# Gated attention and a bilinear feed-forward on one core: the gate applied per token at the end instead of being folded into the feed-forward and the attention sums

## The chip, the core and the metric

One Trainium2 chip, one of its cores. The time is the device time of one execution in microseconds (us), the median of several runs; lower is better. The core has five engines that run their own instruction streams and meet by semaphores: TensorE (PE, matrix products into PSUM), VectorE (DVE), ScalarE (ACT), GpSimd (POOL) and SyncE (SP, which here only issues DMAs).

## The reference

For 2048 tokens of width 512 the output mixes two branches by a sigmoid gate of the token:

```python
x = A_x
g = _sigmoid((x * gate_w).sum(-1, keepdims=True))
a = _A_ref(x, A_wqkv, A_wo)                      # attention, 32 heads of 16
b = _B_ref(x, B_w_gate, B_w_up, B_w_down)        # ((x @ w_gate) * (x @ w_up)) @ w_down
return g * a + (1 - g) * b
```

The feed-forward's inner width F is 1376, eleven column blocks of 128 (the last of 96).

## The kernel before, in words

**Attention.** The queries are cut into four chunks c of 512, the heads into eight groups of four heads per chunk, so there are NG = 32 groups m = (c, b, p), and each has 16 key tiles kt of 128: 512 *entries* (m, kt) of four *heads* each. For a head PE makes 128 keys x 512 queries of scores in one PSUM bank (L950), some engine exponentiates them to bf16, and PE multiplies the four heads of an entry with the values into psO (L1189, "PV"); a column of ones beside the values gives the softmax's denominators. PSUM has eight banks: psS is six of them, used as two slots of three, psO one, psX one; the sixth bank of psS also serves as a second general bank.

**Two engines exponentiate.** ACT takes spans of two or three banks with one Exp (L1551) and writes to a ring PT. DVE takes whole entries whose kt is in DK (five key tiles of a group at most): for each head a clamp to int16 out of PSUM (L1082, four per entry, into a *buffer* of four heads), then four "cheap" passes over the whole buffer (L1111), each giving an approximate exponential at another offset; PE multiplies each of the four with values that POOL has scaled by another weight (VD, and wv once it has been used; L569), so such an entry costs four PVs. Pass k = 3 is written in place, and the buffer is free again when its PV is done. There are two buffers in I2 (part of tile SC) and a third: bsb at first, and wk once the last key projection has read wk (lines with `third`, `bsb_i`, `wk_i`; `nb = (dst["buf"] + 1) % 3` in `d_claim`). No entry goes to DVE before the model time D_START = 38.

**The rest of PE's work is units** (class `Unit`): a chain of matmuls into one general bank and a drain of that bank, mostly by DVE. Units wait in `fills`, sorted by a due time counted in entries begun. There are projections of keys (`mk_k`), queries (`mk_q`), values (`mk_v`), one unit for the gate's 64 tiny products (`mk_gate`, due 16), the feed-forward's `mk_ug` (per chunk c and column block f one unit "u" and one "g", multiplied into hT), and `mk_dw`: for a tile of 128 tokens t of the first three chunks, eleven matmuls of hT with w_down and four of the attention's output OT with wo in one accumulation, drained by one copy to ost (L782) and stored. The last chunk uses `mk_d` (L728, a copy to bsb) and four tail units with `combine` (L747). FFN gives the due times chunk by chunk.

**How the gate gets there.** ACT and DVE make gval = g and omg = 1 - g, [128 x 16], token t*128 + p in partition p and column t. For folding them into operands they must lie along the free dimension, so POOL stores both to DRAM, gsc, one element of 4 bytes at a time (L626, two DMAs of 8 KB), reads g back as gC (L638, eight DMAs) and 1 - g as omgB, broadcast to all partitions, 512 tokens at a time (L587; later chunks from SP). The drain of a "u" unit multiplies by omgB (L674). The softmax's reciprocal denominators are multiplied by gC (L1284, in `finish`), which therefore waits until gC is there.

**The ends of a pair of groups.** `norm` copies psO to oraw (L1244) and issues on SP four DMAs to onum (L1251) and one of the denominators to den (L1261). `finish` lets DVE make reciprocals (L1280), SP write and broadcast them through DRAM into rb (L1294, L1307) and POOL multiply (L1310) into OT; `o_mult` is that product. `mk_q` after its drain (L504) issues eight DMAs on SP (L513), Qst to QX, 16 KB each, which lay the heads' queries apart; the scores of the next head block b wait for them.

**What sets the order.** Nothing reorders at run time: each engine follows its program, and a wait holds all that stands behind it. The program is made ahead by a greedy simulation in the kernel's text (`_Plan`, `step_pe`, `step_act`, `step_dve`) with assumed durations (`dur`, `lat`): at each step PE takes scores, PVs or a unit, DVE takes from `dve_q` by priority what the simulation holds ready, and `d_claim` gives DVE an entry when the simulation finds DVE not too far behind. So how many entries DVE takes follows from how busy the simulation thinks it is.

Of the kernel before, what the change touches and what calls it, by code (L numbers as in the profile page):

```python
# [151 lines left out]
def _build(nc, A_x, A_wqkv, A_wo, W_gate, W_up, W_down, gate_w, out):  # L152
# [10 lines left out]
    NB = 4  # L163
# [5 lines left out]
    D_START = 38.0  # L169
    X_FILL = 45.0  # L170
# [11 lines left out]
    FFN = [(64, 160, 164, 5), (184, 270, 275, 5), (295, 385, 395, 4), (412, 478, 480, 5)]  # L182
# [7 lines left out]
    gsc = nc.dram_tensor("gscr", [2, S], F32, kind="Internal").ap()  # L190

    with ExitStack() as stack:
# [28 lines left out]
        bsb = sb("bsb", [128, 4, D], BF16)  # L221
        omgB = sb("omgB", [128, 512], F32)
        gC = sb("gC", [128, NCH, 32], F32)
# [310 lines left out]
        def mk_v(t, due):  # L534
# [3 lines left out]
            def drain(un, last):  # L538
# [24 lines left out]
                def make():  # L563
                    un.free = P.op("dve", lambda v: v.tensor_copy(vf[:], un.bank), deps, **EV)
                    for k in range(4):
                        dst_ = hc((VV[:, t, :] if k == 0 else vdk(t)[:, k - 1, :])[:, 0 : 17 * H])
                        o = P.op(
                            "pool",
                            lambda g, k=k, dst_=dst_: g.tensor_scalar(dst_, hd(vf[:]), _WT[k], None, ALU.mult),  # L569
                            [un.free, o_vd, o_one],  # L570
                            dur=1.3,
                        )
                        if k == 0:
                            ev_v[t] = o
                    ev_vd[t] = o
# [5 lines left out]
        ogate, o_omg, gate_wait = {}, {}, []  # L581

        def ld_omg(c, deps, eng="sp"):

            o_omg[c] = P.dma(
                eng,
                lambda e: e.dma_start(omgB[:], bass.AP(gsc.tensor, gsc.offset + S + 512 * c, [[0, 128], [1, 512]])),  # L587
                deps,
                f"domg{c > 0}",
            )  # L590


        def mk_gate(due):
# [13 lines left out]
            def drain(un, last):  # L607
                def amake():
                    e1 = un.free = P.op(
                        "act",  # L610
                        lambda a: a.activation(gex[:], un.bank[:, 0:T], ACT.Exp, scale=-1.0),
                        [last],
                        dur=0.1,
                        lat=0.15,
                    )

                    def make():
                        e2 = P.op("dve", lambda v: v.tensor_single_scalar(gden[:], gex[:], 1.0, ALU.add), [e1])
                        e3 = P.op("dve", lambda v: v.reciprocal(gval[:], gden[:]), [e2], dur=0.2)
                        ogate["g"] = P.op(  # L620
                            "dve", lambda v: v.tensor_scalar(omg[:], gval[:], -1.0, 1.0, ALU.mult, ALU.add), [e3]
                        )
                        for i, src_ in enumerate([gval, omg]):
                            o = P.dma(
                                "pool",
                                lambda e, i=i, src_=src_: e.dma_start(  # L626
                                    gsc[i].rearrange("(t p) -> p t", p=128), src_[:], allow_slow_non_contiguous=True
                                ),
                                [ogate["g"]],
                                "dgs",  # L630
                                dur=1.0,
                                lat=20.0,
                            )
                        for i in range(8):
                            p, j = i % 2, i // 2
                            o1 = P.dma(
                                "pool",
                                lambda e, p=p, j=j: e.dma_start(  # L638
                                    gC[32 * j : 32 * j + 32, :, 16 * p : 16 * p + 16],
                                    bass.AP(gsc.tensor, gsc.offset, [[16, 32], [512, NCH], [1, 16]]),  # L640
                                ),
                                [o],
                                "dgc",
                                dur=1.0,
                            )
                        ogate["c"] = o1
                        for dl in gate_wait:
                            dl[-1] = o1
                        ld_omg(0, [o], "pool")

                    dve_push(3, [e1], make)

                act_q.append(([last], amake))
# [3 lines left out]
        def mk_ug(c, f, which, due):  # L657
# [9 lines left out]
            def drain(un, last):  # L667
                if which == "u":
                    deps = [last, u_free.get(n - 2), o_omg[c]]

                    def make():
                        ev_u[n] = un.free = P.op(
                            "dve",
                            lambda v: v.tensor_tensor(usb[0:w, n % 2, :], un.bank[0:w, :], omgB[0:w, :], ALU.mult),  # L674
                            deps,
                            **EV,
                        )
                        if f == FT - 1 and c < NCH - 1:
                            ld_omg(c + 1, [un.free])
# [18 lines left out]
            def deps():  # L698
                r = [d_wu if which == "u" else d_wg] + xdep(c)
                if which == "u":  # L700
                    r.append(o_omg[c])
# [12 lines left out]
        def mk_d(c, tt, due):  # L714
# [6 lines left out]
            def drain(un, last):  # L721
# [3 lines left out]
                deps = [last, last_v.get("b")]  # L725

                def make():
                    ev_b[t] = un.free = P.op("dve", lambda v: v.tensor_copy(bsb[:, tt, :], un.bank), deps, **EV)  # L728
# [3 lines left out]
            def deps():  # L732
                r = [d_wd] + [ev_h[c, f] for f in range(FT)]
                return r
# [5 lines left out]
        def combine(t, bank, last, un=None, dst=None):  # L740
# [3 lines left out]
            def make():  # L744
# [3 lines left out]
                        dst, bank, gval[:, t : t + 1], bsb[:, t % 4, :], ALU.mult, ALU.add  # L748
# [16 lines left out]
        def mk_dw(c, tt, due):  # L765

            t = 4 * c + tt

            def mm(pe, bk, i, s0, s1):
                if i < FT:  # L770
                    w = FW[i]
                    return cmm(pe, bk, hT[0:w, i, tt * 128 : (tt + 1) * 128], wd[0:w, i, :], s0, s1)
                b = i - FT
                return cmm(pe, bk, OT[:, c % 2, b, tt * 128 : (tt + 1) * 128], wo[:, b, :], s0, s1)

            def drain(un, last):
                if tt == 3:
                    ot_use[c] = h_use[c] = last
                deps = [last, o_out.get(t - 2)]

                def make():
                    o_comb[t] = un.free = P.op("dve", lambda v: v.tensor_copy(ost[:, t % 2, :], un.bank), deps, **EV)  # L782
                    o_out[t] = P.dma(
                        "sp",
                        lambda e: e.dma_start(out2[t * 128 : (t + 1) * 128, :], ost[:, t % 2, :]),
                        [o_comb[t]],
                        f"dout{t % 2}",
                    )

                dve_push(2, deps, make)  # L790

            def deps():
                r = [d_wd, d_wo] + [ev_h[c, f] for f in range(FT)] + [o_mult[c, b] for b in range(NB)]
# [4 lines left out]
            return Unit(due, chain(FT + NB, mm), deps, drain)  # L798
# [87 lines left out]
        def cap(sl, now):  # L886


            if sl and not xs[1]["res"] and now > X_FILL:
# [102 lines left out]
        bsb_i = bsb[:, :, :].bitcast(I16)  # L992
        third = {}

        def i2b(e):


            return I2[:, on_d[e], :, :] if on_d[e] < 2 else third[e]
# [10 lines left out]
        def d_claim(now):  # L1009
            if now < D_START or not last_x or tails or l_state["n"] > D_CHEAP:  # L1010
                return False
            nb = (dst["buf"] + 1) % 3
# [21 lines left out]
            if nb == 2:  # L1034
                third[g, kt] = wk_i if "k" in last_v else bsb_i
# [33 lines left out]
        def d_unit(j, bank, o, h):  # L1069
# [5 lines left out]
            d4 = [o, d_free[nb] or (last_x[0] if nb < 2 else None)]  # L1075
            if nb == 2 and third[e] is wk_i:
                d4.append(last_v["k"])

            def make():
                x = P.op(  # L1080
                    "dve",
                    lambda v: v.tensor_scalar(i2b(e)[:, j, :], bank, _LO, _HI, ALU.max, ALU.min),  # L1082
# [14 lines left out]
        def cheap(e, nb):  # L1097
# [5 lines left out]
            def mk(k):  # L1103
                lf = l_free[k] if k < 3 else None

                def make():
                    src = i2b(e)[:, :, :].rearrange("p a b -> p (a b)")
# [44 lines left out]
        def lview(e, k, j):  # L1152
            nb = on_d[e]
            return (LL[:, k, j, :] if k < 3 else i2b(e)[:, j, :]).bitcast(BF16)
# [11 lines left out]
        def do_pv(it):  # L1166
# [45 lines left out]
            if isd:  # L1212
                if k == 3:
                    nb = on_d[e]
                    d_free[nb] = o
                    if nb == 2 and third[e] is bsb_i:
                        last_v["b"] = o
# [57 lines left out]
        def finish(blk, c, b, dd, nd, half):  # L1275
# [3 lines left out]
            def make():  # L1279
                r = P.op("dve", lambda v: v.reciprocal(rec[:, s, 0:w_], den[:, s, 0:w_]), dd + [norm_ops.get(("scr", blk - 2))], dur=0.25)  # L1280
                if c < NCH - 1:
                    r = P.op(
                        "dve",
                        lambda v: v.tensor_tensor(rec[:, s, 0:w_], rec[:, s, 0:w_], gC[:, c, 0:w_], ALU.mult),  # L1284
                        [r, ogate["c"]],
                    )
# [30 lines left out]
            dl = dd + [ogate.get("c", "pending")]  # L1317
            if "c" not in ogate:
                gate_wait.append(dl)
            dve_push(1, dl, make)  # L1320


# [5 lines left out]
        fl.append((16, mk_gate(16)))  # L1328
# [8 lines left out]
        for c, (a0, a1, ad, dd) in enumerate(FFN):  # L1337
            for f in range(FT):
                for i, w in enumerate("ug"):
                    du = a0 + (a1 - a0) * (2 * f + i) / (2 * FT)  # L1340
                    fl.append((du, mk_ug(c, f, w, du)))
            for tt in range(4):
                du = ad + dd * tt
                fl.append((du, (mk_dw if c < NCH - 1 else mk_d)(c, tt, du)))
# [74 lines left out]
        def step_pe():  # L1419
# [41 lines left out]
            if xi is not None:  # L1461
                f = pick_fill(t + 0.3)
                if t > X_FILL and any(isinstance(x["u"], Unit) for x in xs):
# [215 lines left out]
```

## Time and profile before

| | |
|---|---|
| median of 3 runs | 779.12 us (777.76 to 781.05) |
| the profiled execution's own time | 779.12 us |
| its span, first to last instruction | 777.4 us (1.7 us lie around it) |
| mean granted TensorE clock | 0.968 of full |
| busy: PE, DVE, ACT, POOL | 715.6, 697.9, 729.7, 75.1 us |
| ACT's Exp, 128x1024 and 128x1536 | 434 and 235 times, mean 1074 and 1500 ns |
| DVE's clamps (L1082) and cheap passes (L1111) | 464 and 464 times, mean about 690 and 710 ns |
| DMA moved | 23.95 MB in 33745 packets, 20756 of them under 512 B |

The heads divide into 464 on DVE (116 entries) and 1584 on ACT. The mean of an instruction is longer than its share of time when the next one begins before it ends: in a row of DVE's 128x512 drains starts lie 0.60 us apart, at a mean duration of about 0.69 us. In a timeline row the two numbers are the start and the duration in us; the bracket at the end is the engine's idle time before it and what released it. SPq is the SP engine's issuing of DMAs.

### The profile page before, as it was taken

The numbers are of one execution on the slowest core, as the hardware profiler recorded it, in microseconds if no ns is written. First come the engines' busy times: TensorE is split into PE (matmuls) and PEld (weight loads), VectorE is DVE, ScalarE is ACT, GpSimd is POOL, SyncE is SP. The second block draws the span as 40 slices with busy tenths as digits, with TensorE's granted clock in tenths as the row PEclk, the third lists the DMA queues.
The fourth block names the chain that finished last, engine by engine and source line by source line (L and its number), as shares of the span: only waits on it lengthen the run. The fifth ranks groups of instructions, "written<-read, shape, count | busy, mean of one in ns | idle before, by whom it ended". The sixth has DMA issues, their size and how long they took to land.

```text
span 777.4 us, 21121 instructions
## 1 busy us (share of the span) xinstructions
PE 715.6 (92%) x8982; PEld 212.3 (27%) x8982; DVE 697.9 (90%) x1164; ACT 729.7 (94%) x680; POOL 75.1 (10%) x84
## 2 busy tenths in 40 slices
PE   9993898999899899999999999999887999999997
PEld 3330222222222222222222222222221322222234
DVE  3382999999999899999998999999998999999865
ACT  6982999999999989999998999999997999999995
POOL 8862000000001000000000000000000000000000
PEclk9986999999999999999997999999998999999999
DMA  8863010001010010101001010000101001000001
GB/s 175 272 11 23 8 30 13 17 11 30 9 29 22 16 30 22 30 8 24 16 11 35 14 40 19 23 17 9 27 18 29 16 23 32 14 19 14 24 11 42
DMA packets 33745, 23.95 MB, mean 31 GB/s; under 512 B 20756, under 2 KB 27988, under 8 KB 33652
## 3 DMA queue, kind: packets, MB, share of 16 engines
q1 hardware_dynamic: 31908, 21.21, 11.9%
q0 software_dynamic: 688, 1.13, 1.0%
q8 instruction: 72, 1.18, 0.7%
q10 hardware_dynamic: 1056, 0.26, 0.2%
q14 instruction: 21, 0.17, 0.1%
HBM read 12.35 MB, written 2.37 MB: 19 GB/s over the span
## 4 chain that ended last, share of the span: by engine, by line
DVE 41%; PE 34%; ACT 12%; DMA 4%; SPq 3%; issue 3%; POOL 1%; DVEq 0%; ACTq 0%
DVE SC L1111 15%; ACT PT L1551 12%; PE psS L950 11%; DVE SC L1082 11%; PE psX L374 10%; PE psO L1189 10%; DVE wk L1082 5%; SPq L1251 3%; DVE usb L674 2%; DMA den<-oraw 2%; DMA QX<-Qst 2%; DVE hT L691 2%; DVE oraw L1244 1%; DVE bsb L1082 1%; PE psS L374 1%
## 5 line engine op out<-in xcount | busy, mean ns | idle before, releaser
L1551 ACT ACTIVATE PT<-psS 128x1024 bf16<-128x1024 f32 (+1 forms) x670 | 721.9, 1222 | 32.3 <-PE psS L950 26.5
L950 PE MATMUL psS<-QX,KT 32*128 32x512 bf16 x1991 | 274.0, 391 | 39.1 <-ACT PT L1551 15.2
L1111 DVE TENSOR_SCALAR SC<-SC 128x2048 int16<-128x2048 int16 x308 | 206.3, 709 | 4.4 <-remote 2.4
L1082 DVE TENSOR_SCALAR SC<-psS 128x512 int16<-128x512 f32 x273 | 183.0, 687 | 17.4 <-PE psS L950 16.7
L950 PEld LDWEIGHTS psS<-QX,KT 32*128 32x128 bf16 x1991 | 69.5, 91 | 303.7 <-ACT PT L1551 86.2
L1189 PE MATMUL psO<-PT,VV 128*32 128x512 bf16 x1518 | 147.9, 393 | 1.1 <-DVE oraw L1244 0.6
L1189 PE MATMUL psO<-SC,VD 128*32 128x512 bf16 x1208 | 115.0, 395 | 6.2 <-DVE SC L1111 5.3
L1310 POOL TENSOR_TENSOR OT<-onum,rb 128x512 bf16<-128x512 f32 x16 | 23.4, 1464 | 664.0 <-DMA rb<-rscr 664.0
L1082 DVE TENSOR_SCALAR wk<-psS 128x512 int16<-128x512 f32 x113 | 75.8, 687 | 6.0 <-PE psS L950 5.5
L1111 DVE TENSOR_SCALAR SC<-wk 128x2048 int16<-128x2048 int16 x96 | 64.4, 689 | 2.9 <-PE psS L1199 1.6
L374 PE MATMUL psX<-wd,hT 128*32 128x512 bf16 (+1 forms) x704 | 57.8, 392 | 2.4 <-DVE ost L782 1.9
L374 PE MATMUL psX<-xT,wu 128*32 128x512 bf16 x688 | 53.1, 388 | 1.1 <-DVE wk L1082 0.5
L374 PE MATMUL psX<-xT,wg 128*32 128x512 bf16 x688 | 52.8, 388 | 0.7 <-DVE SC L1082 0.2
L1189 PEld LDWEIGHTS psO<-PT,VV 128*32 128x32 bf16 x1518 | 38.2, 96 | 53.6 <-issue 39.8
L1189 PE MATMUL psO<-SC,VV 128*32 128x512 bf16 x456 | 45.6, 390 | 1.2 <-DVE SC L1111 0.9
L1189 PEld LDWEIGHTS psO<-SC,VD 128*32 128x32 bf16 x1208 | 29.9, 95 | 58.7 <-DVE SC L1111 32.9
L691 DVE TENSOR_TENSOR hT<-psX,usb 128x512 bf16<-128x512 f32 (+1 forms) x44 | 30.2, 686 | 0.7 <-PE psX L374 0.7
L674 DVE TENSOR_TENSOR usb<-psX,omgB 128x512 bf16<-128x512 f32 (+1 forms) x44 | 30.2, 687 | 0.2 <-PE psX L374 0.2
L1082 DVE TENSOR_SCALAR SC<-psX 128x512 int16<-128x512 f32 x35 | 24.0, 687 | 0.8 <-PE psX L1052 0.6
L1111 DVE TENSOR_SCALAR wk<-wk 128x2048 int16<-128x2048 int16 x32 | 23.9, 747 | 0.0
L1244 DVE COPY oraw<-psO 128x512 f32<-128x512 f32 x31 | 21.3, 688 | 0.7 <-PE psO L1189 0.7
L1052 PE MATMUL psX<-QX,KT 32*128 32x512 bf16 x55 | 21.6, 393 | 0.1
(131 smaller groups left out, 399.7 us busy)
## 6 DMA issues: line engine op xcount, KB each, us to landing
rb<-rscr SPq DMA_DIRECT2D x16, 256.0 KB
onum<-oraw SPq DMA_DIRECT2D x124, 32.0 KB, 2.0
QX<-Qst SPq DMA_DIRECT2D x120, 16.0 KB, 1.8
out_dram<-ost SPq DMA_DIRECT2D x12, 128.0 KB, 1.7
wu<-in_B_w_up_dram SPq DMA_DIRECT2D x1, 1376.0 KB, 7.0
wg<-in_B_w_gate_dram SPq DMA_DIRECT2D x1, 1376.0 KB, 9.9
wd<-in_B_w_down_dram SPq DMA_DIRECT2D x1, 1280.0 KB, 12.5
omgB<-gscr SPq DMA_DIRECT2D x3, 256.0 KB, 3.4
```

Of the source, the lines that this page charges most:

```text
L374: r = pe.matmul(dst_[j : j + 32, :], lhs[:, j : j + 32], rhs, start=s0, stop=s1, tile_position=(0, j), skip_group_check=True,)
L674: lambda v: v.tensor_tensor(usb[0:w, n % 2, :], un.bank[0:w, :], omgB[0:w, :], ALU.mult),
L691: lambda v: v.tensor_tensor(hT[0:w, f, :], un.bank[0:w, :], usb[0:w, n % 2, :], ALU.mult),
L950: q = pe.matmul(bank_ap(sl, k_), KT[32 * j : 32 * j + 32, b, kt * 128 : (kt + 1) * 128], QX[32 * j : 32 * j + 32, p, b, :], start=True, st ...
L1052: lambda pe: pe.matmul(bank, KT[32 * j : 32 * j + 32, b, kt * 128 : (kt + 1) * 128], QX[32 * j : 32 * j + 32, p, b, :], start=True, stop=True,
L1082: lambda v: v.tensor_scalar(i2b(e)[:, j, :], bank, _LO, _HI, ALU.max, ALU.min),
L1111: lambda v: v.tensor_scalar(dstt, src, 0.5, _BASE + _OFF[k], ALU.mult, ALU.add),
L1189: r = pe.matmul(psO[r_, :], vcol(m, kt, k_, j), pj, start=first, stop=last, tile_position=(0, 32 * j), skip_group_check=True)
L1244: o_ev[m] = P.op("dve", lambda v: v.tensor_copy(oraw[:, s, :], psO[:]), deps, **EV)
L1251: lambda e, r0=r0: e.dma_start(onum[r0 : r0 + 16, :], oraw[r0 : r0 + 16, s, :]),
L1310: lambda g: g.tensor_tensor(OT[:, c % 2, b, :], onum[:], rb[:], ALU.mult),
L1551: lambda a: a.activation(cell_ap(cells[0], n).rearrange("p a b -> p (a b)"), bank_ap(sl, 0, n), ACT.Exp, scale=_LN2 / _OCT,),
```

## The change

The gate is no longer folded into operands. gsc, gC, omgB, their DMAs, the multiplication by gC and the wait for it are gone. The drain of "u" is a plain copy. Every chunk uses `mk_d`, whose drain multiplies by 1 - g, taken per token from omg, into bsb, now a ring of five tiles; for the first three chunks a new unit `mk_wo` multiplies OT with wo (four matmuls), and `combine` drains it as gval * bank + bsb into ost. With it go: bsb is no third buffer for DVE's entries, so there are two until wk is free; D_START is 45 in place of 38 (X_FILL, from which the second general bank is given up, stays at 45 under that name); the gate unit is due at 20 in place of 16; the feed-forward's due times are spread evenly from 60 to 490; the simulation's assumed duration of POOL's value scaling (L569) is 0.75 in place of 1.3.

```diff
-    D_START = 38.0
-    X_FILL = 45.0
+    D_START = 45.0
...
-    FFN = [(64, 160, 164, 5), (184, 270, 275, 5), (295, 385, 395, 4), (412, 478, 480, 5)]
+    FFN_FROM, FFN_TO = 60.0, 490.0
...
-    gsc = nc.dram_tensor("gscr", [2, S], F32, kind="Internal").ap()
...
-        bsb = sb("bsb", [128, 4, D], BF16)
-        omgB = sb("omgB", [128, 512], F32)
-        gC = sb("gC", [128, NCH, 32], F32)
+        bsb = sb("bsb", [128, 5, D], BF16)
...
-                            dur=1.3,
+                            dur=0.75,
...
-                        for i, src_ in enumerate([gval, omg]):
-                            o = P.dma(
-                                "pool",
-                                lambda e, i=i, src_=src_: e.dma_start(
-                                    gsc[i].rearrange("(t p) -> p t", p=128), src_[:], allow_slow_non_contiguous=True
-                                ),
-                                [ogate["g"]],
...
-                        for i in range(8):
-                            p, j = i % 2, i // 2
-                            o1 = P.dma(
-                                "pool",
-                                lambda e, p=p, j=j: e.dma_start(
-                                    gC[32 * j : 32 * j + 32, :, 16 * p : 16 * p + 16],
...
-                        ld_omg(0, [o], "pool")
...
-                    deps = [last, u_free.get(n - 2), o_omg[c]]
+                    deps = [last, u_free.get(n - 2)]
...
-                            lambda v: v.tensor_tensor(usb[0:w, n % 2, :], un.bank[0:w, :], omgB[0:w, :], ALU.mult),
...
+                            "dve", lambda v: v.tensor_copy(usb[0:w, n % 2, :], un.bank[0:w, :]), deps, **EV
...
-                deps = [last, last_v.get("b")]
+                deps = [last, ogate["g"], b_use.get(t - 5)]
                 def make():
-                    ev_b[t] = un.free = P.op("dve", lambda v: v.tensor_copy(bsb[:, tt, :], un.bank), deps, **EV)
+                    ev_b[t] = un.free = P.op(
+                        "dve",
+                        lambda v: v.tensor_scalar(bsb[:, t % 5, :], un.bank, omg[:, t : t + 1], None, ALU.mult),
+                        deps,
+                        dur=0.65,
+                        lat=0.1,
+                    )
...
-        def mk_dw(c, tt, due):
+        def mk_wo(c, tt, due):
             t = 4 * c + tt
-            def mm(pe, bk, i, s0, s1):
-                if i < FT:
-                    w = FW[i]
-                    return cmm(pe, bk, hT[0:w, i, tt * 128 : (tt + 1) * 128], wd[0:w, i, :], s0, s1)
-                b = i - FT
+            def mm(pe, bk, b, s0, s1):
                 return cmm(pe, bk, OT[:, c % 2, b, tt * 128 : (tt + 1) * 128], wo[:, b, :], s0, s1)
             def drain(un, last):
                 if tt == 3:
-                    ot_use[c] = h_use[c] = last
-                deps = [last, o_out.get(t - 2)]
...
+                    ot_use[c] = last
+                combine(t, un.bank, last, un)
             def deps():
-                r = [d_wd, d_wo] + [ev_h[c, f] for f in range(FT)] + [o_mult[c, b] for b in range(NB)]
+                r = [d_wo, ev_b[t]] + [o_mult[c, b] for b in range(NB)]
...
-            return Unit(due, chain(FT + NB, mm), deps, drain)
+            return Unit(due, chain(NB, mm), deps, drain)
...
-            nb = (dst["buf"] + 1) % 3
+            nb = (dst["buf"] + 1) % (3 if "k" in last_v else 2)
...
-                if c < NCH - 1:
-                    r = P.op(
-                        "dve",
-                        lambda v: v.tensor_tensor(rec[:, s, 0:w_], rec[:, s, 0:w_], gC[:, c, 0:w_], ALU.mult),
-                        [r, ogate["c"]],
-                    )
...
-        fl.append((16, mk_gate(16)))
+        fl.append((20, mk_gate(20)))
...
-        for c, (a0, a1, ad, dd) in enumerate(FFN):
+        n_ffn = NCH * (2 * FT + 4)
+        a0, a1 = FFN_FROM, FFN_TO
+        q = 0
+        for c in range(NCH):
             for f in range(FT):
-                for i, w in enumerate("ug"):
-                    du = a0 + (a1 - a0) * (2 * f + i) / (2 * FT)
+                for w in "ug":
+                    du = a0 + (a1 - a0) * q / n_ffn
                     fl.append((du, mk_ug(c, f, w, du)))
+                    q += 1
             for tt in range(4):
-                du = ad + dd * tt
-                fl.append((du, (mk_dw if c < NCH - 1 else mk_d)(c, tt, du)))
+                du = a0 + (a1 - a0) * q / n_ffn
+                fl.append((du, mk_d(c, tt, du)))
+                q += 1
+        for c in range(NCH - 1):
+            fl += [(128 * (c + 1) + 8 + 3 * tt, mk_wo(c, tt, 128 * (c + 1) + 8 + 3 * tt)) for tt in range(4)]
```

## The prediction, on record before the changed kernel ran

> **What bounds the kernel now.** I began with the page: busy times, then the 40 slices.
>
> ```profile
> span 777.4 us, 21121 instructions
> PE 715.6 (92%) x8982; PEld 212.3 (27%) x8982; DVE 697.9 (90%) x1164; ACT 729.7 (94%) x680; POOL 75.1 (10%) x84
> ...
> DVE  3382999999999899999998999999998999999865
> ACT  6982999999999989999998999999997999999995
> PEclk9986999999999999999997999999998999999999
> ```
>
> Three engines are near full. The digits say where they are not: the filling, the tail, and one hole in slice 4 (58 to 78 us), where both DVE and ACT stand at 2 and the clock at 6. Outside, DVE and ACT share the exponentials and are full together, so work added to DVE is paid by giving ACT heads. So two questions: what makes the hole, and what does the change do to the balance?
>
> For the hole I took the timelines by engine, then the waits from 58 to 80 us.
>
> ```profile
> 51.37 1.16 POOL L626 DMA_DIRECT2D gscr<-omg  x1
> ...
> 53.81 5.01 SPq L513 DMA_DIRECT2D QX<-Qst  x8
> ...
> 70.25 0.57 POOL L638 DMA_DIRECT2D gC<-gscr  x1 [17.73 <-DMA gscr<-omg]
> ...
> 71.64 0.61 PE L950 MATMUL psS<-QX,KT 32*128 32x512 bf16 x3 [12.28 <-DMA QX<-Qst]
> ```
>
> ```profile
> 61.72 1.45 ACT L1551 ACTIVATE PT<-psS 128x1536 bf16<-128x1536 f32 x1 [3.10 <-remote]
> 72.30 1.02 ACT L1551 ACTIVATE PT<-psS 128x1024 bf16<-128x1024 f32 x1 [9.13 <-PE psS L950]
> 74.24 1.02 ACT L1551 ACTIVATE PT<-psS 128x1024 bf16<-128x1024 f32 x1 [0.92 <-PE psS L950]
> 75.76 1.94 ACT L1551 ACTIVATE PT<-psS 128x1024 bf16<-128x1024 f32 x2 [0.50 <-PE psS L950]
> ```
>
> PE waits 12.28 us for the queries of head block 1, the eight small DMAs of SP. ACT and DVE starve behind it. How long do these DMAs take elsewhere? The answer on the tile Qst:
>
> ```profile
> L513 SPq DMA_DIRECT2D QX<-Qst x120: 512/589/1678, 53.8 to 701.8; - x120
> ...
> DMA to landing us min/median/max: 1.7/1.8/13.8
> ```
>
> Median 1.8 us, but 13.0 to 13.8 us for these eight. What is different is just ahead of them: POOL's two stores of the gate to DRAM at 50.1 and 51.4 us, 4096 elements of 4 bytes, which land at 70.25. In the table of 2 us windows the DMA share, under 0.1 before, is 0.87 at 52 us and 2.50 at 56 us while 14 GB/s are moved: packets stand open and carry almost nothing. I read the hole as the price of folding the gate: the store clogs the engines that the queries need.
>
> **Part 1: the stores, reads and broadcasts of the gate go.** What the hole costs, on ACT: 3.10 + 9.13 + 0.92 + 0.50 = 13.65 us idle from 58.61 to 75.76 (the last two because PE restarts at a granted clock of 0.50 after the hole). On DVE the same stretch has 2.40 + 9.76 + 0.65 + 0.83 = 13.64. The 3.10 and 2.40 are put down to "remote", no instruction of the program; both end within 0.13 us of each other, inside the jam, so I count them. What is late next: the last of the eight is issued at 58.24; at the median 1.8 it lands at 60.0, and PE stood ready at 59.36. In the new order the gate unit is due after this query unit (20, not 16), which brings Qst forward by up to the 4 us that the gate's products take (42.2 to 46.5), so the wait may vanish. I keep 0.5. **-13.1** (from -13.65 to, if the stores are not the cause, 0).
>
> The Trainium skill, "DMA: Bandwidth & Descriptors", section "Queues, rings and completion order", says on one side that a DMA engine serves its queues in turn, a packet at a time, by which eight copies of 16 KB would only share with the stores; then the 12.28 would have another cause, and the sum below would be 786.5. The same section says that a completion increment lands only after all earlier writes of that engine, across queues, by which the copies wait for the scatter to finish. The trace is nearer to the second: from 67 to 70 us the DMA share is 0.00, yet stores and copies complete at 70.25 and 71.51.
>
> **Part 2: DVE's added work.** From the groups by shape:
>
> ```profile
> L782 DVE CAST ost<-psX 128x512 bf16<-128x512 f32 x12 | 8.2, 685 | 0.0
> L1284 DVE TENSOR_TENSOR rec<-rec,gC 128x32 f32<-128x32 f32 x12 | 2.3, 192 | 0.4
> L747 DVE SCALAR_TENSOR_TENSOR hT<-psS,gval,bsb 128x512 bf16<-128x512 f32 x3 | 2.1, 741 | 0.0
> L486 DVE TENSOR_SCALAR QX<-psX,mask 128x512 bf16<-128x512 f32 x1 | 0.8, 752 | 1.9 <-ACT QX L477 1.9
> ```
>
> In a row drains start 0.60 us apart at a mean of 0.685; so I take 0.60 for a copy, 0.665 for the multiplying drain with a column of scalars (L486's form) and 0.655 for the combining one (L747's). Twelve copies to ost go (7.2) and twelve of L1284 (2.3); twelve multiplying (8.0) and twelve combining (7.9) come, and the last chunk's four drains grow by 0.065 (0.3). L674 (687 ns) turns into a copy, no gain. Sum: **+6.7 us of DVE**. PE's matmuls are the same in number.
>
> What is a us of DVE worth? An entry costs DVE four clamps and four passes at 0.60, 4.8 us; on ACT it costs 4 x 0.457 = 1.83 (about 724 us of Exp over 1584 heads). If DVE loses x, it gives up n entries until both end together: x - 4.8n = 1.83n. The end moves by 1.83/6.63 = **0.276 x**. So +6.7 gives **+1.8**. The cover is that ACT takes what DVE drops; without it, all 6.7.
>
> **Part 3: DVE begins later.** The first clamp is at 40.30 now, with D_START 38; with 45, some 7 us later. Until 47.3 DVE does nine such instructions (seven clamps, two passes): 5.4 us x 0.276 = **+1.5** (0 if later slack takes them).
>
> **Part 4: the third buffer is missing until wk is free.** bsb holds 28 clamps and 28 passes, 7 entries from 44 to 178 us; the first in wk is at 185.8. From 80 to 185 DVE has nearly no idle time (19.96, 19.96, 18.96, 20.00, 19.96 of 20 from 80 to 180). A buffer is held some 11 us (first clamp of one at 112.2, last pass at 122.4, then its PV), and the three now begin an entry each 5.5 us. Two buffers held 11 us also give one each 5.5 us, if nothing slips; things do, as a buffer must wait for its group's turn in psO. Ends: 0, and all 7 entries lost, 33.6 us x 0.276 = 9.3. I take two of seven, nearer to the arithmetic of 11 us: 9.6 x 0.276 = **+2.6**.
>
> **Part 5: what the order gets wrong.** Rows of POOL's scaling last 1.49 us; the simulation assumes 0.75 instead of 1.3. PE then comes earlier to values that are not there: with 1.3 PE lost 0.26 us once, for the VV of the fourth scaled tile. The copy it reads ends at 35.29, so with 0.75 it is simulated to end at 36.1 at the earliest, against 37.68 in the trace: at most 1.5 us, and ACT has a span in hand. I take **+0.5** (0 to 1.5). The new unit of OT and wo is due 8 entries after its chunk, where the old one came 11 to 36 after; it waits for POOL's product, behind the chain den, rec, rscr, rb. Behind it on PE stand scores and PVs. The trace has no wait on OT. The nearest rows are the waits of DVE's reciprocal for den, 13.1 us in 11 times, the longest 3.9. Three chunks: from -2 (such waits may also get fewer in a new order) to +10; **+1.0**, nearer to the short waits. The POOL DMAs and omgB loads hold nothing else up: POOL waits for rb 664 us of the span.
>
> **Sum**, against the profiled execution, whose own 779.12 us (span 777.4, 1.7 around it) is also the median: -13.1 + 1.8 + 1.5 + 2.6 + 0.5 + 1.0 = -5.7: **773.4 us**. Without the hole the bound is what it is elsewhere: DVE and ACT full together.
>
> **Rivals.** *A: the gain is eaten.* For: parts 3 and 4 both fall in the first 185 us, where only DVE's entries relieve ACT; if all seven entries go, +9.3 in place of +2.6 makes 780.1, no measurable change. Against: wk comes at the same due time, and 11 us of holding allow two buffers to keep up. *B: slower, by the unit of OT and wo.* Twice the trace shows what a late den does to PE: gaps of 1.87 us at 271 and 2.83 at 590, each followed by a clock of 0.50 for 3 to 7 us, and ACT idle 3.1 and 3.9 in all. If PE runs into POOL's product, one such gap, at the longer price, for each of three chunks is 3 x 3.9 = 11.7; in place of the +1.0 that is 784.1, over the line of 0.5%. It decides when the product is more than some 2 us later than simulated at all three chunk ends. For: the simulation takes 0.3 us for a DMA issue on SP that lasts 0.59, and a query unit is due at the same place. Against: older due units go first. *C: the hole stays,* the change not doing what it removes: if the copies were slow for themselves, 786.5. Against: the median of all 120 is 1.8.
>
> **Chances.** Forecast 0.61, A 0.20, B 0.12, C 0.07. I call 0.5% (3.9 us: 775.2 to 783.0) what a measurement can tell. The forecast case gives faster 0.57 and same 0.04; A faster 0.02, same 0.17, slower 0.01; B and C slower. So faster 0.59, same 0.21, slower 0.20. Range: the good end takes -13.65, +1.8, nothing for parts 3 and 4, 0 and -2: 765.3, and 766 for the little chance that all come together; the bad end reaches past A to B's 784; C and the worst of B, under 2 in 10, are left out.
>
> **What would show it.** Right: no hole near 60 us, ACT and DVE digits of 8 or 9 there; the QX copies' longest landing near 2 us; DVE 12 multiplying drains and 12 combining ones more; entries on DVE 112 or 113 instead of 116; DVE idle in the windows of 80 to 180 by about 10 us. Wrong: a gap near 60 us with another releaser (the copies still 13 us: C); DVE entries below 110 (A); PE waits on POOL's OT after entries 128, 256 and 384 with the clock at 0.5 (B). New stops in the order, which no row here can show, would make all of it wrong.

## The result, and the profile after

The changed kernel takes 768.97 us (median of 4 runs, 768.81 to 773.14) against 779.23 for the one before: ratio 0.988, 95% interval 0.9841 to 0.9919. In a second series (k10 below) it is 772.25 against 779.85, ratio 0.9904 (0.9866 to 0.9942). So it is faster by some 8 to 10 us, about 1%; the forecast was 5.7, inside a range of 766 to 784. The profiled execution took 768.81, 1.8 us more than its span. One of the six executions of k1, below, took 1373.67 us, and k1's numbers leave it out.

The page after, the lines that answer to those of before:

```profile
span 767.0 us, 21248 instructions
PE 713.1 (93%) x9054; PEld 215.5 (28%) x9054; DVE 701.6 (91%) x1164; ACT 728.9 (95%) x678; POOL 67.4 (9%) x73
...
DVE  3349999989999999999989999999999799999996
ACT  6989999999999999999989999999999799999994
PEclk9978799999999999999999999999999899999999
```

ACT's busy time hardly moved (729.7 to 728.9) and DVE's rose by 3.7: the whole gain is idle time that went. The 2s in slice 4 are gone. What stands in their place, in ACT's timeline:

```profile
52.26 1.02 ACT L1484 ACTIVATE PT<-psS 128x1024 bf16<-128x1024 f32 x1 [0.38 <-PE psS L895]
...
55.05 1.02 ACT L1484 ACTIVATE PT<-psS 128x1024 bf16<-128x1024 f32 x1 [0.78 <-PE psX L991]
56.99 4.38 ACT L1484 ACTIVATE PT<-psS 128x1024 bf16<-128x1024 f32 x4 [0.91 <-PE psS L895]
62.19 26.54 ACT L1484 ACTIVATE PT<-psS 128x1536 bf16<-128x1536 f32 x23 [0.82 <-PE psS L895]
```

Small stops under a low clock (0.55 of full from 48 to 52 us, 0.50 to 62), no wait for query copies, no "remote". And the query copies, on the tile Qst:

```profile
L509 SPq DMA_DIRECT2D QX<-Qst x120: 507/589/1818, 44.7 to 679.4; - x120
...
DMA to landing us min/median/max: 1.7/1.8/3.3
```

The first is issued at 44.7 instead of 53.8 (the gate unit now comes after the query unit), and the longest lands in 3.3 us instead of 13.8.

**An account of the spans.** Adding up the idle times in the brackets of ACT's timeline from 16 us on gives ACT's *stops*; the span less these is the *rest*. "Heads" is how many heads DVE exponentiates (count of clamps). k1 to k13 are the experiments below. Each number is of one profiled execution:

| kernel | span | ACT's stops | rest | heads on DVE |
|---|---|---|---|---|
| before | 777.4 | 29.8 | 747.6 | 464 |
| changed, first series / k10 | 767.0 / 771.2 | 19.9 / 23.0 | 747.1 / 748.2 | 464 |
| k1: before, stores side by side | 764.7 | 16.6 | 748.1 | 464 |
| k9 / k11: fold without the jam | 760.2 / 767.4 | 12.7 / 19.2 | 747.5 / 748.2 | 464 |
| k12: the same, SP's issues simulated longer | 754.2 | 7.1 | 747.1 | 464 |
| k2: before, gate unit at 20 | 775.5 | 26.6 | 748.9 | 468 |
| k3: changed, gate at 16, with the stores | 786.5 | 34.0 | 752.5 | 460 |
| k4: the same without the stores | 770.5 | 20.8 | 749.7 | 460 |
| k5: changed, FFN windows of before | 769.5 | 19.7 | 749.8 | 456 |
| k7 / k8: changed, D_START 38 / third buffer | 770.8 / 770.3 | 21.0 / 21.4 | 749.8 / 748.9 | 464 |
| k13: changed, FFN_TO 491 | 766.7 | 15.5 | 751.2 | 460 |

The rest stays within 747 to 753 us. By the way it is made it is ACT's busy time (727.7 to 732.3 us in these executions) and the ends of the span, so it says that ACT's work hardly differs between these kernels; the stops do, from 7.1 to 34.0. The hole was 13.65 of the 29.8 of before. From 50 to 90 us ACT's stops sum to 15.3 us before and to 3.8 and 3.4 in the changed kernel's two series; outside they sum to 14.5 before and to 16.0 and 19.6 after.

One execution tells a kernel's stops only roughly: k9 and k11 are the same program, and their stops differ by 6.5 us.

### The profile page after: what moved, and what is told of

The parts are those of the page before. It is cut to its first block, busy times and chain, and to the rows that moved or that the text cites. A ratio compares the mean times of both kernels' runs of the same rounds, so it can differ in the third digit from the quotient of the medians.

```text
span 767.0 us, 21248 instructions
## 1 busy us (share of the span) xinstructions
PE 713.1 (93%) x9054; PEld 215.5 (28%) x9054; DVE 701.6 (91%) x1164; ACT 728.9 (95%) x678; POOL 67.4 (9%) x73
## 3 DMA queue, kind: packets, MB, share of 16 engines
q1 hardware_dynamic: 31476, 20.42, 10.4%
## 4 chain that ended last, share of the span: by engine, by line
DVE 40%; PE 28%; ACT 20%; issue 4%; SPq 3%; DMA 3%; POOL 1%; DVEq 0%; POOLq 0%; ACTq 0%
ACT PT L1484 20%; DVE SC L1048 15%; DVE SC L1019 12%; PE psS L895 9%; PE psX L370 8%; PE psO L1126 7%; DVE wk L1019 5%; SPq L1186 3%; DVE usb L632 2%; DMA den<-oraw 2%; DVE hT L645 2%; DVE oraw L1179 1%; DVE wk L1048 1%; PE psO L1136 1%; PE psS L370 1%
## 5 line engine op out<-in xcount | busy, mean ns | idle before, releaser
L895 PE MATMUL psS<-QX,KT 32*128 32x512 bf16 x1984 | 271.8, 390 | 28.3 <-ACT PT L1484 15.5
L1048 DVE TENSOR_SCALAR SC<-SC 128x2048 int16<-128x2048 int16 x332 | 219.4, 701 | 0.8 <-PE psO L1126 0.4
L1019 DVE TENSOR_SCALAR SC<-psS 128x512 int16<-128x512 f32 x284 | 190.2, 686 | 13.7 <-PE psS L895 12.2
L1126 PE MATMUL psO<-PT,VV 128*32 128x512 bf16 x1526 | 149.5, 392 | 1.5 <-POOL VV L565 0.7
L1019 DVE TENSOR_SCALAR wk<-psS 128x512 int16<-128x512 f32 x116 | 77.9, 687 | 0.9 <-PE psS L895 0.8
L1048 DVE TENSOR_SCALAR SC<-wk 128x2048 int16<-128x2048 int16 x99 | 69.0, 717 | 0.6 <-PE psO L1126 0.5
L370 PE MATMUL psX<-wd,hT 128*32 128x512 bf16 (+1 forms) x704 | 56.1, 386 | 0.2 <-DVE bsb L683 0.2
L1019 DVE TENSOR_SCALAR SC<-psX 128x512 int16<-128x512 f32 x48 | 32.9, 686 | 1.3 <-PE psS L895 1.2
L632 DVE CAST usb<-psX 128x512 bf16<-128x512 f32 (+1 forms) x44 | 30.1, 685 | 0.8 <-PE psX L370 0.8
L991 PE MATMUL psX<-QX,KT 32*128 32x512 bf16 x64 | 25.4, 398 | 1.4 <-DVE usb L632 0.6
## 6 DMA issues: line engine op xcount, KB each, us to landing
wd<-in_B_w_down_dram SPq DMA_DIRECT2D x1, 1280.0 KB, 13.1
```

The lines of the kernel that those rows point to most:

```text
L370: r = pe.matmul(dst_[j : j + 32, :], lhs[:, j : j + 32], rhs, start=s0, stop=s1, tile_position=(0, j), skip_group_check=True,)
L632: "dve", lambda v: v.tensor_copy(usb[0:w, n % 2, :], un.bank[0:w, :]), deps, **EV
L895: q = pe.matmul(bank_ap(sl, k_), KT[32 * j : 32 * j + 32, b, kt * 128 : (kt + 1) * 128], QX[32 * j : 32 * j + 32, p, b, :], start=True, st ...
L991: lambda pe: pe.matmul(bank, KT[32 * j : 32 * j + 32, b, kt * 128 : (kt + 1) * 128], QX[32 * j : 32 * j + 32, p, b, :], start=True, stop=True,
L1019: lambda v: v.tensor_scalar(i2b(nb)[:, j, :], bank, _LO, _HI, ALU.max, ALU.min),
L1048: lambda v: v.tensor_scalar(dstt, src, 0.5, _BASE + _OFF[k], ALU.mult, ALU.add),
```

## Experiments

### Is it the stores? One layout, same order: k1

```diff
-  gsc[i].rearrange("(t p) -> p t", p=128), src_[:], allow_slow_non_contiguous=True
+  gsc[i].rearrange("(p t) -> p t", p=128), src_[:]
```

> The kernel before with one line changed: the two stores of the gate to DRAM put each partition's 16 values side by side (128 runs of 64 bytes) instead of 2048 single elements; every engine's program is the same, only the stores' layout differs, so the tokens' gates arrive permuted. Theory S (the stores of single elements jam the DMAs that the queries need): the hole at 59 to 76 us is gone, the longest landing of the query copies falls from 13.8 to under 4 us, and the time falls by 12 to 14 us, to 765 to 767. Rival O (the hole comes from where the gate unit and the query unit stand in the order, or from the eight small copies themselves): nothing changes, 779, the landing stays near 13 us.

Measured 767.52 against 778.92, ratio 0.9867 (0.9828 to 0.9906). The page and the tile Qst of k1:

```profile
PE 713.7 (93%) x8982; PEld 211.6 (28%) x8982; DVE 696.4 (91%) x1164; ACT 729.7 (95%) x680; POOL 73.4 (10%) x84
```

```profile
L513 SPq DMA_DIRECT2D QX<-Qst x120: 507/589/1854, 53.8 to 689.8; - x120
...
DMA to landing us min/median/max: 1.7/1.8/3.8
```

The copies are issued at the same 53.8 us, behind the same instructions, and land in 3.8 us at most. All engines run the same instructions in the same order as before; only the gates reach other tokens, so k1 measures time and is no kernel to use. So theory S holds: it is the 4096 single elements, not the place of the units or the copies themselves. Their price, 11.4 us by the medians and 10.4 by the ratio, is a little under the 12 to 14 expected: ACT's stops from 50 to 90 us still sum to 5.2.

### Would moving the gate unit have been enough? k2

```diff
-        fl.append((16, mk_gate(16)))
+        fl.append((20, mk_gate(20)))
```

> The kernel before with the gate unit due at 20 instead of 16, everything else as it is, the stores of single elements too. By theory S the query copies are now issued before the stores and land in 2 to 4 us, so this hole goes too; the stores then lie over whatever DMA comes next (the first pair's sums), which nothing waits for before some 90 us: 765 to 769. Rival O says the same for another reason, 765 to 769; a rival by which the fold itself costs (the chain through DRAM, wherever it stands) says 775 to 780. It tells how much of the changed kernel's gain a move of one unit alone would have brought.

Measured 776.91 against 778.92, ratio 0.9985 (0.9959 to 1.0012): no difference that can be told, and a miss for theory S as I had put it. The query copies do go ahead and land in 3.4 us. But the waits from 50 to 86 us show another victim:

```profile
POOL gC L638 <- DMA gscr<-omg: 16.9, 1, 16.9
...
PEld psX L374 <- DVE KT L408: 4.6, 1, 4.6
...
DVE KT L408 <- remote: 4.3, 1, 4.3
...
PE psX L374 <- DVE KT L408: 4.1, 1, 4.1
...
ACT PT L1551 <- remote: 1.6, 1, 1.6
```

DVE and ACT stop for something that is no instruction of the program, both until 70.3 us, and PE waits for DVE; no query copy was in flight. The table of DMA queues has the candidate, a queue "instruction". In 57 to 75 us of k2 its one packet holds 1.8% of 16 engines for 18 us:

```profile
q0 software_dynamic: 96, 0.02, 10.4%
q8 instruction: 1, 0.02, 1.8%
```

That is 0.018 x 16 x 18 = 5.2 us for a packet of about 16 KB. In k4, a kernel without the stores (next section), it is 0.9 (from 52 to 70 us):

```profile
q1 hardware_dynamic: 461, 0.21, 5.1%
q14 instruction: 2, 0.02, 0.3%
q8 instruction: 1, 0.02, 0.3%
```

So packets of instructions also take longer beside the stores. And the "remote" stops come from the stores: they stand in before, k2 and k3, the three kernels with single-element stores, and in no other, k1 included, whose order is that of before. That ACT and DVE ran out of instructions is inferred, and the times fit only in part. In k2 the packet lasts from 64.2 to 69.5 us and the waits end at 70.3. In k3 (next section) the packet of q8 begins at 64.2, just when the waits end; the one that ends ahead of that, at 63.7, is of q14 and has 8 KB. In the kernel before the waits end at 61.72 and 61.85, and the nearest packet, of q14, at 62.4. No run took a packet away by itself, so what the engines waited for stays open.

Moving a unit also changes the order that the simulation makes: DVE has 468 heads in k2. ACT's stops from 50 to 90 us fall from 15.3 to 10.0 us, and outside they rise from 14.5 to 16.6. So the 2 us are not the price of the move alone.

### The stores put into the changed kernel: k3, beside k4

```diff
-        fl.append((20, mk_gate(20)))
+        fl.append((16, mk_gate(16)))
...
+  for i, src_ in enumerate([gval, omg]):              # k3 only; k4 has the line above alone
+      P.dma("pool", lambda e, i=i, src_=src_: e.dma_start(
+          gsc[i].rearrange("(t p) -> p t", p=128), src_[:], allow_slow_non_contiguous=True), [ogate["g"]], "dgs", dur=1.0, lat=20.0)
```

> The changed kernel with the gate unit back at 16 and the two stores of single elements put back behind it, which nobody reads. Theory S: the hole comes back, query copies land after 12 to 14 us, 779 to 783, some 12 us above the same kernel without the stores. Rival O: the same time as the same kernel without the stores.

> The changed kernel with the gate unit back at 16 and no stores. Theory S: no hole, the copies land in under 4 us, 768 to 772 as the changed kernel (769). Rival O (the unit's place makes the hole): 779 to 783, with PE waiting for the query copies near 60 us.

Measured 784.92 for k3 (ratio 1.0091, 1.0057 to 1.0125) and 774.62 for k4 (0.9963, 0.9934 to 0.9991): two stores that nobody reads cost 10.3 us. In k3, from its timelines by engine:

```profile
64.26 1.94 ACT L1496 ACTIVATE PT<-psS 128x1024 bf16<-128x1024 f32 x2 [3.43 <-remote]
```

```profile
73.39 0.61 PE L907 MATMUL psS<-QX,KT 32*128 32x512 bf16 x3 [2.91 <-DMA QX<-Qst]
```

The last query copy there is issued from 59.37 to 60.07 us and PE gets it at 73.39, 14.0 us after that issue began; in the kernel before it was 13.4 (58.24 to 71.64). The profile tells no landing times for these eight copies, and the 2.9 us that the tile Qst of k3 gives as the longest is of others, so this goes by PE's wait. k4 has neither line, and its engines run in the order of k3. So from both sides, taking the stores away and putting them in, the jam is worth 10 to 11 us. Both kernels are above the times expected of them, k4 by 5 us above the changed kernel without any jam; this was not foreseen and belongs to the next questions.

### What the added work costs: k5, k7, k8

My terms for the added drains, the later start and the missing buffer came to +5.9, by way of heads going to ACT. But DVE has 464 heads before and after. Where did it find the time? Clamps alone in the last 80 us, in the window tables of k1 and then of the changed kernel (columns: window, length, DVE busy with clamps and their count, granted clock, DMA share, GB/s):

```profile
685.00:766.00 81.00, 19.99 (x30) 0.98 0.08 22
```

```profile
687.00:768.00 81.00, 30.32 (x47) 0.98 0.07 20
```

47 heads against 30: DVE falls behind by 16 or 17 heads up to 687 us and makes them up in the tail, where DVE of k1 is busy 59.0 of some 80 us and that of the changed kernel 71.8. One thing that frees it is the even spread of due times, which leaves few feed-forward drains there. So I put the old windows back into the changed kernel (k5), and undid parts 3 and 4 by themselves.

```diff
-    FFN_FROM, FFN_TO = 60.0, 490.0
+    FFN = [(64, 160, 164, 5), (184, 270, 275, 5), (295, 385, 395, 4), (412, 478, 480, 5)]
```

> The changed kernel with the feed-forward's due times of before (FFN: chunk by chunk, the last chunk's from 412 to 478 and 480 to 495). Theory E: what the prediction's cost terms missed is the tail; the even due times leave few drains there, so DVE takes 47 heads in the last 80 us where it took 31 in the kernel with side-by-side stores, and that gives back the heads which the added drains cost earlier. Then here the heads on DVE in the last 80 us fall to 30 to 35, all DVE heads from 464 to about 448, and the time rises by 2 to 5 us, to 771 to 774. Rival F (the terms of the prediction's parts 2 to 4 are simply too large, the due times do nothing): 464 heads and 768 to 770.

```diff
-    D_START = 45.0
+    D_START = 38.0
+    X_FILL = 45.0
```

> The changed kernel with D_START 38 again, X_FILL left at 45 (part 3 of the prediction undone). By the prediction's price 1.5 us less: 767.5. By theory E the tail returns what the start loses: 769, equal within what can be told. A new order alone moved the time by some 5 us when the gate unit was moved (774.6 against 769), so anything from 766 to 775 can come from the order.

```diff
-            nb = (dst["buf"] + 1) % (3 if "k" in last_v else 2)
+            nb = (dst["buf"] + 1) % 3
...
+                third[g, kt] = wk_i if "k" in last_v else bsb_i
```

> The changed kernel with bsb as the third buffer again until wk is free (part 4 undone). By the prediction's price 2.6 us less: 766.4, with DVE's idle time from 80 to 180 us falling from 5 us to about 1. By theory E 768 to 769. By the order alone 766 to 775.

k5 does with the heads what theory E says:

```profile
690.00:771.00 81.00, 21.73 (x33) 0.99 0.07 20
```

33 in the tail, 456 in all where about 448 were expected, and ACT's busy time goes from 728.9 (729.1 in k10) to 732.3: 8 heads for 3.2 to 3.4 us, 0.40 to 0.43 each where I had taken 0.457. But the time does not rise: 769.46 against 782.24 on that chip, ratio 0.9838 (0.98 to 0.9875), if anything below the changed kernel's 0.988. So theory E is shown for the heads, and its price for the end is a miss. k7 gives 0.9856 (0.9824 to 0.9888), k8 0.9877 (0.9846 to 0.9907), with DVE idle for 2.4 us from 80 to 180 us where about 1 was expected: neither part shows a price that these runs can tell from nothing. Nor do they refute the prices of 1.5 and 2.6 us: the intervals reach some 2.5 us to either side, and the changed kernel itself was not run beside these.

### The order's luck: k10 and k13

> The changed kernel itself, unchanged, on the chip of the next three, as their reference: a ratio of 0.988 to the kernel before, as measured first (0.9841 to 0.9919).

```diff
-    FFN_FROM, FFN_TO = 60.0, 490.0
+    FFN_FROM, FFN_TO = 60.0, 491.0
```

> The changed kernel with FFN_TO 491 in place of 490, a change without meaning, to see what a new order alone does. If an order's luck is small, within 1.5 us of the changed kernel; if the differences of 2 to 6 us between variants of the changed kernel are such luck, 2 us or more away, to either side.

Measured on one chip: k10 772.25 (0.9904, 0.9866 to 0.9942), k13 764.92 (0.9814, 0.9769 to 0.9859). The edit moves the end of the feed-forward's spread, and with it each of its due times by at most one entry; the kernel is 7.3 us faster, although DVE does four heads fewer. The two profiled executions are 4.5 us apart: the stops differ by 7.5 (23.0 and 15.5), the rest by 3.0 the other way. Two of the changed kernel's stops make up most of the 7.5; ACT's timeline in the first series (in k10 they are 2.90 and 4.11 us):

```profile
402.75 1.02 ACT L1484 ACTIVATE PT<-psS 128x1024 bf16<-128x1024 f32 x1 [2.68 <-PE psS L895]
```

```profile
598.53 1.45 ACT L1484 ACTIVATE PT<-psS 128x1536 bf16<-128x1536 f32 x1 [4.13 <-PE psS L895]
```

and what stood behind them, DVE's timeline and PE's:

```profile
400.77 0.35 DVE L1215 RECIPROCAL rec<-den 128x32 f32<-128x32 f32 x1 [3.42 <-DMA den<-oraw]
```

```profile
595.98 1.90 PE L370 MATMUL psX<-wo,OT 128*32 128x512 bf16 x16 [3.30 <-POOL OT L1239]
```

The second is rival B, at one of its three places: the new unit of OT and wo stands on PE before POOL's product is there. In the 2 us windows the clock is at 0.64, 0.50, 0.50 and 0.65 from 594 to 602 us. k13 has no stop over 1.5 us after the filling.

### Folding without the jam: k9, k11; and a better order: k12

```diff
-  xT[:, kt, t * 128 : (t + 1) * 128],
+  xT[:, kt, t:S:16] if t < T else xT[:, kt, 1536 + 128 * (t - T) : 1664 + 128 * (t - T)],
...
-  gsc[i].rearrange("(t p) -> p t", p=128), src_[:], allow_slow_non_contiguous=True
+  gsc[i].rearrange("(p t) -> p t", p=128), src_[:, 0:T]
```

> The kernel before, gate folded, with the gate's products taken over tokens 16p + t instead of 128t + p, so that both stores are 128 runs of 64 bytes in the right order; four more columns give the last chunk's tokens as before (80 tiny products in place of 64); all else and the order as before. Theory S: as fast as the kernel with permuted side-by-side stores, 766 to 769, no hole, query copies landing in under 4 us. If the strided weight reads of the gate's products are slow, 1 to 3 us more. Rival O: 779.

> The folded kernel with side-by-side stores in the right order once more, beside the changed kernel. If folding without the jam is truly cheaper than not folding, it is 4 us or more below the changed kernel here too (first measured: 0.9786 of before, against 0.988). If the two are equal once the jam is gone, they are within 3 us of each other.

> The same folded kernel with the ordering model told what an issue on SP lasts: 0.6 in place of 0.3 for the query copies and the copies to onum (the trace: 0.59). Theory W: the remaining stops are DVE waiting for den, 12.7 us in 11 times, with PE idle and a low clock behind some; a better order loses 3 to 6 us of them: 760 to 763. Rival: a new order only brings other stops, within 4 us of the same kernel without it.

k12's edit:

```diff
-  dur=0.3,      # the copies Qst to QX, and oraw to onum
+  dur=0.6,
```

k9: 765.89, ratio 0.9786 (0.9749 to 0.9823). Its strided gate products take PE 5.2 us (80 of them) where the 64 of before take 2.4; the time is at the lower end of what was expected, so it shows no price of that. k11, the same kernel on the chip of k10: 767.36, ratio 0.9837 (0.9792 to 0.9883), so 4.9 us below the changed kernel there, with intervals that overlap a little. k12: 761.11, ratio 0.9758 (0.9706 to 0.981), the fastest of all. The waits of k11 and then of k12:

```profile
ACT PT L1551 <- PE psS L950: 17.6, 28, 2.0
...
DVE rec L1280 <- DMA den<-oraw: 13.6, 10, 3.9
```

```profile
DVE rec L1280 <- DMA den<-oraw: 6.9, 3, 3.5
...
ACT PT L1551 <- PE psS L950: 6.5, 16, 1.0
```

With issues simulated as long as they last (0.59 in the trace), DVE's waits for den fall from 10 to 3, and ACT's for scores from 17.6 us to 6.5. The time is as theory W had it, 6.3 us below k11. But one order was tried, and k13's 7.3 us show that one order can jump as far for no reason; among the other orders DVE's waits for den go from 7.7 us (k13) to 20.4 (k4). So that the longer durations are the cause is not shown.

## The prediction, point by point

**The hole and its cause: right.** k1, k3 and k4 show the stores as the cause, at 10 to 11 us where I took 13.1. In the changed kernel ACT's stops from 50 to 90 us fall by 11.5 (11.9 in k10): small stops stay in the place of the hole, which the term had not left. What I counted on a guess, the "remote" stops, turned out to be a second effect of the same stores: k2 has it without the first. Rival C is refuted by k1. The Trainium skill, "DMA: Bandwidth & Descriptors", section "Queues, rings and completion order", left two readings, sharing by turns and a completion that waits for earlier writes. All eight copies landed late alike, 13.0 to 13.8 us after their issue, also the first of them; they needed at most 3.8 behind side-by-side stores, and k2's copies, issued ahead, at most 3.4. That is nearer to the second reading, but no run here separates the two.

**"Brings Qst forward": right.** Qst is drained at 43.9 us against 49.8, and no wait for the copies is left; the 0.5 that I kept was not needed for it.

**Parts 2, 3 and 4, together +5.9: the mechanism failed.** The step was "if DVE loses x, it gives up n entries until both end together". DVE gave up none in the end: 16 or 17 heads up to 687 us, all made up in the last 80. Only part 3 had named this cover ("0 if later slack takes them"), as an end of its range; I had read in the page that DVE's digits fall to 6 and 5 in the tail, and did not ask whether the simulation would fill them. ACT's time for a head is about as I took it (0.40 to 0.43 us in k5 against 0.457), but k5, which does give up 8 heads, is no slower, so that the end moves with the heads is not shown either. The predicted shape, 112 or 113 entries, is refuted: 116. DVE's drains cost what I took: means of 745 ns for the multiplying and 745 for the combining ones, in the rows that I went by 752 and 741. DVE's idle time from 80 to 180 us is 5.1 us (before 1.1) where I said 10.

**Part 5: right in kind, and the place where the order's cost is.** PE's waits for POOL's values were 1.0 us in two times against 0.3 before (predicted 0.5 more). Of rival B's three gaps one came, at somewhat more than the price put on it: ACT idle 4.13 + 0.49 + 0.27 = 4.9 us against 3.9. The other large stop, at 401 us, is the wait for den that the kernel before has elsewhere.

**The sum.** With the jam gone in both, the unfolded kernel is slower than the folded one: by 4.9 us on one chip (k10 against k11); by the ratios to the kernel before, across chips, it is anything from 1 us (0.988 against k1's 0.9867) to 9 (0.9904 against k9's 0.9786). The prediction had +7.4 for parts 2 to 5. That is more than the 4.9 and inside the wider span, but its split is wrong: the number of heads did not change, and what is seen is stops. Outside the hole's place the changed kernel has 1.5 and 5.1 us more of them than before. So the saving (13.1 against 11.5) and the costs (7.4 against these) were both taken too large, with opposite signs; that the sum came within 5 us is partly luck. What none of my terms had is the size of an order's luck, 7.3 us for due times moved by at most one entry. The range of 766 to 784 held the time, though it had no term for this; the nearest neighbour of the changed kernel (k13, 764.92) lies outside it. Whether unfolding costs anything by itself stays open: each kernel is one order.

## What to carry to other kernels

Here two DMAs of 8 KB, made of single elements of 4 bytes, stopped ACT, DVE and PE for some 10 us: look in the profile not for a DMA's bytes but for other transfers that land late beside it, and lay the data out so that it leaves in runs (here by choosing which tokens a product's rows are). Where the program's order comes from a simulation, a time of one variant is a draw; compare at a fixed order where that can be had, as k1 did, and count the main engine's stops, in more than one execution. Telling such a simulation the durations that the trace shows, those of DMA issues too, is worth a try: the one order made so (k12) was the fastest here.

## What the runs showed of the hardware

Two stores of 2048 elements of 4 bytes each, SBUF to DRAM, issued in 2.4 us, kept copies of 16 KB waiting 13 us instead of 1.8 (the kernel before), and a packet of 16 KB of instructions took about 5 us instead of 0.9 to 1.4 (before, k2 and k3 against k1 and k4); the DMA share of the kernel before was 0.00 from 67 to 70 us, just before the stores landed. And the granted clock fell to 0.50 without a long gap of PE: in the kernel before at 366 us after three windows of 2 us in which PE was busy 1.87, 1.75 and 1.53, its waits each under 0.3 us; it stayed there for some 3 us.
